# Column sums of squares as three bf16 parts, and a half tile of tokens filled up with zero rows, in a fused attention and feed-forward kernel

## The chip, the cores and the metric

The kernel runs on one core of one Trainium2 chip. Its time is the device time of one execution in microseconds (us). A profile shows the span from the first to the last instruction, which is some 1.8 us shorter than that time. PE is the tensor engine, PEld its weight loads, DVE the vector engine, ACT the scalar engine, POOL GpSimd, SP the engine that issues most DMAs.

## The reference, cut to what matters

```python
B, N, C = 4, 6080, 256
qn = q / (np.linalg.norm(q, axis=1, keepdims=True) + 1e-06)   # norm over the 6080 tokens, for each channel
kn = k / (np.linalg.norm(k, axis=1, keepdims=True) + 1e-06)
s = kn.transpose(0, 2, 1) @ qn / tau                          # 256 x 256 per batch
a = softmax(s)                                                # over the last axis
x = (v @ a).reshape(B * N, C)
out = gelu_tanh(x @ w_in) @ w_out                             # 256 -> 2048 -> 256
```

6080 tokens are 47 tiles of 128 and one of 64. That last one is the "half tile".

## The kernel before

The program runs in slots. In a slot PE does four matmuls of 512 columns (`hp`, the hidden layer), eight of 256 columns (`yp`, the output), and then one step of the attention of the next batch, from a Python generator: `yield` ends a step. So the attention of batches 1 to 3 hides nothing by itself; it is woven into the PE stream of the batch before. The parts that the change touches:

```python
def col_sums(cols, x, ones, first, last):
    for m in range(4):                       # q and k, two halves of 128 channels each
        nc.tensor.matmul(cols[:, m : m + 1],
                         lhsT=x[m // 2][:, m % 2 * 128 : m % 2 * 128 + 128], rhs=ones, ...)

def attention_steps(b, aw_next):
    ...
    for n, ch in enumerate(later_chunks):
        load_qk(b, n + 2)
        qk, whole = loaded_of.pop((b, n))
        for s, rows in slots_of(ch):         # rows: 128, or 64 for the half tile
            gram(G, qk, s, rows, first, last)              # two matmuls of 256 columns: G += k^T q
            flat = whole[:rows, :, s, :]
            ...                              # DVE: sq = flat * flat (bf16), acc += sq (fp32)
            yield
            ...
    cols = pA.tile([128, 512], FP32, tag="a", name="cols")
    col_sums(cols, [acc[:, x] for x in range(2)], ones_f, True, True)     # fp32 weights
    r = ...                                  # DVE copy; POOL: square root
    yield; yield; yield
    ...                                      # DVE: 1/norm; Gs = G scaled, fp32
    yield; yield
    T = turned(Gs)                           # four fp32 transposes on PE
    ...                                      # ACT: th; then per half jc, DVE: den, eT[jc]
    yield; yield
    rsinv = row_sums(eT)                     # rs: four matmuls of one column
    ...                                      # eight aw_part, one per slot
```

## Time and profile before

| What | Before |
|---|---|
| Time, median of the first 3 runs | 756.42 us (756.24 to 757.38) |
| PE busy in the stretch 41 to 712 us | 670.95 of 671.00 us |
| Slot with a gram of 128 rows / with the half tile | 1.96 / 2.16 us |
| fp32 column sums, per batch, on the PE stream | 0.81 us |
| DVE busy, ACT busy | 37%, 56% |

PE has no idle time in the middle of the run, so the only question for any change there is for how long it holds the PE stream. Such a hold is read from the distance of two starts in the timeline, not from the durations, which overlap. The lines are in the prediction below.

### The profile page before, as it was taken

What the parts mean: (1) busy time and instruction counts of PE and PEld (TensorE: products, weight loads), DVE (VectorE), ACT (ScalarE), POOL (GpSimd) and SP (SyncE); (2) the same over time, 40 slices, a digit from 0 to 9 for tenths busy, and PEclk for the clock granted to TensorE, in tenths of its full rate; (3) what the DMA queues carried; (4) which work ended last, traced back from release to release, by engine and by line L of the source; (5) the groups of instructions that cost most, each with busy time, mean ns of one, the idle gap of its engine ahead of it and who ended that gap; (6) DMA issues with size and microseconds to landing.
All of it is one profiled execution on the core that took longest, in us unless ns stands there. A gap on an engine that the chain in (4) does not pass through costs nothing.

```text
span 754.2 us, 12371 instructions
## 1 busy us (share of the span) xinstructions
PE 733.3 (97%) x5262; PEld 503.5 (67%) x5262; DVE 277.5 (37%) x485; ACT 420.3 (56%) x411; POOL 75.6 (10%) x150
## 2 busy tenths in 40 slices
PE   2999999999999999999999999999999999999998
PEld 1656666776666666776666666766767666666666
DVE  3733556454401546554521265555441011011011
ACT  4875555555456555555555555555546655555552
POOL 1311111101012102101001102010101000000000
PEclk9999999999999999999999999999999999999999
DMA  9999685615147685813435776661513543322111
GB/s 368 346 190 156 103 150 137 118 43 83 48 93 143 114 161 108 162 52 60 99 57 118 140 117 121 148 133 46 83 43 80 96 95 74 69 74 54 41 56 57
DMA packets 79639, 83.59 MB, mean 111 GB/s; under 512 B 55392, under 2 KB 59104, under 8 KB 79072
## 3 DMA queue, kind: packets, MB, share of 16 engines
q0 software_dynamic: 17104, 32.97, 27.4%
q1 hardware_dynamic: 62176, 48.20, 23.8%
q10 hardware_dynamic: 304, 1.64, 0.5%
q8 instruction: 41, 0.67, 0.4%
q14 instruction: 14, 0.11, 0.0%
HBM read 78.91 MB, written 24.90 MB: 138 GB/s over the span
## 4 chain that ended last, share of the span: by engine, by line
PE 94%; DMA 4%; ACT 1%; issue 0%; DVE 0%; SPq 0%; POOL 0%; DVEq 0%
PE yp L510 44%; PE hp L584 44%; PE G L157 4%; PE ps L217 2%; ACT sq L268 1%; DMA st<-in_q_dram 1%; DMA st<-in_k_dram 1%; DMA win_bf<-in_moe_w_in_dram 1%; PE cols L169 0%; PE yp L615 0%; PE T L195 0%; DVE aw L404 0%; PE vps L422 0%; PE ps L384 0%; PE rs L204 0%
## 5 line engine op out<-in xcount | busy, mean ns | idle before, releaser
L588 ACT ACTIVATE g<-hp 128x1024 bf16<-128x1024 f32 (+1 forms) x384 | 389.8, 1015 | 308.2 <-PE hp L584 308.2
L510 PE MATMUL yp<-wout_bf,g 128*128 128x256 bf16 x3024 | 392.0, 273 | 0.0
L584 PE MATMUL hp<-vT,aw 128*128 128x512 bf16 (+1 forms) x1536 | 390.8, 377 | 0.2 <-DVE aw L404 0.2
L510 PEld LDWEIGHTS <-g 128*128 128x128 bf16 x3024 | 295.9, 98 | 113.4
L584 PEld LDWEIGHTS <-aw 128*128 128x128 bf16 x1536 | 149.9, 98 | 104.7 <-issue 0.6
L527 DVE COPY ysb<-yp 128x512 f32<-128x512 f32 (+1 forms) x95 | 64.9, 683 | 402.5 <-PE yp L510 402.5
L451 DVE TENSOR_TENSOR acc<-acc,sq 128x512 f32<-128x512 f32 (+1 forms) x141 | 97.5, 692 | 4.8
L450 DVE TENSOR_TENSOR sq<-qkb 128x512 bf16<-128x512 bf16 (+1 forms) x141 | 58.7, 417 | 0.0
L157 PE MATMUL G<-qkb 128*128 128x256 bf16 (+1 forms) x288 | 55.0, 273 | 0.0
L308 POOL DMA_DIRECT2D vb<-in_v_dram x47 | 25.8, 551 | 76.6 <-DMA vT<-vb 64.3
L226 DVE TENSOR_SCALAR aw<-ps,rsinv 128x512 bf16<-128x512 f32 x30 | 22.4, 749 | 27.1 <-PE ps L217 26.7
L157 PEld LDWEIGHTS <-qkb 128*128 128x128 bf16 (+1 forms) x288 | 27.9, 98 | 3.8 <-issue 0.6
L333 POOL CAST gate<-g 1x1 f32<-1x1 bf16 x24 | 5.9, 244 | 237.3 <-ACT g L588 237.3
L157 PE MATMUL G<-qk 128*128 128x256 bf16 x96 | 13.7, 301 | 15.6 <-DVE qk L266 15.6
L268 ACT ACTIVATE sq<-st 128x3072 bf16<-128x3072 f32 (+2 forms) x9 | 21.1, 2379 | 11.2 <-DMA st<-in_q_dram 8.2
L157 PEld LDWEIGHTS <-qk 128*128 128x128 bf16 x96 | 9.9, 108 | 19.0 <-DVE qk L266 16.6
L266 DVE CAST qk<-st 128x3072 bf16<-128x3072 f32 (+2 forms) x10 | 14.2, 1437 | 13.2 <-DMA st<-in_q_dram 10.0
L217 PE MATMUL ps<-win_bf,eT 128*128 128x512 bf16 x60 | 17.7, 379 | 0.0
L461 POOL TENSOR_TENSOR r<-r,half 128x4 f32<-128x4 f32 x3 | 3.1, 1043 | 113.8 <-DVE r L460 113.8
L81 POOL DMA_DIRECT2D qkb<-in_q_dram x24 | 12.8, 535 | 6.8 <-issue 4.7
L81 POOL DMA_DIRECT2D qkb<-in_k_dram x24 | 12.9, 538 | 0.0
L567 POOL COPY g<-gr 128x1024 bf16<-128x1024 bf16 x2 | 2.1, 1036 | 105.1 <-PE yp L510 105.1
(69 smaller groups left out, 100.7 us busy)
## 6 DMA issues: line engine op xcount, KB each, us to landing
out_dram<-ysb SPq DMA_DIRECT2D x44, 512.0 KB, 2.9
vb<-in_v_dram POOLq DMA_DIRECT2D x43, 256.0 KB, 6.8
qkb<-in_q_dram POOLq DMA_DIRECT2D x21, 384.0 KB, 4.7
qkb<-in_k_dram POOLq DMA_DIRECT2D x21, 384.0 KB, 6.5
st<-in_q_dram SPq DMA_DIRECT2D x2, 1536.0 KB, 11.8
vT<-vb SPq DMA_TRANSPOSE x184, 3.0
st<-in_k_dram ACTq DMA_DIRECT2D x1, 1536.0 KB, 10.3
st<-in_k_dram SPq DMA_DIRECT2D x1, 1536.0 KB, 16.7
```

What stands on the lines that cost most here:

```text
L81: engines[x].dma_start(out=dst[x][:, 0:size, :], in_=src[b, s0 * 128 : (s0 + size) * 128, :].rearrange("(p s) c -> p s c", s=size))
L157: nc.tensor.matmul(G[:, ic, :], lhsT=qk[1][:rows, s, ic * 128 : ic * 128 + 128], rhs=qk[0][:rows, s, :], start=first and ic == 0, stop=las ...
L217: nc.tensor.matmul(ps, lhsT=eT[:, jc, ic * 128 : ic * 128 + 128], rhs=win_bf[:, jc, fs * 512 : fs * 512 + 512], start=jc == 0, stop=jc == 1)
L226: nc.vector.tensor_scalar_mul(dst, ps, scale)
L268: nc.scalar.activation(sq, x, AF.Square)
L308: nc.gpsimd.dma_start(out=t[:, 0:n, :], in_=v_rows[r0 : r0 + n * 128, :].rearrange("(p s) c -> p s c", s=n))
L450: nc.vector.tensor_mul(sq[:rows], flat, flat)
L451: nc.vector.tensor_add(acc[:rows], acc[:rows], sq[:rows])
L510: nc.tensor.matmul(yp[:rows, at, :], lhsT=g[:, fc, s * 128 : s * 128 + rows], rhs=wout_bf[:, fc, :], start=fc == 0, stop=fc == FC - 1)
L527: nc.vector.tensor_copy(ysb[:, s0 : s + 1, :], yp[:, 0 : s + 1 - s0, :])
L584: nc.tensor.matmul(hp[:, j, :cols], lhsT=aw[:, cc, fc * 128 : fc * 128 + 128], rhs=vT[:, cc, :cols], start=cc == 0, stop=cc == 1)
L588: nc.scalar.activation(g[:, 2 * i : 2 * i + 2, :cols], hp[:, :, :cols], AF.Gelu_apprx_tanh)
```

## The change

The intent: PE gets no fp32 weights for the column sums of batches 1 to 3. The fp32 sum `acc` is split into three bf16 numbers that add up to it, each is summed in bf16, and PSUM adds the three. Two empty slots give DVE time for the split. The half tile gets 64 zero rows, so that all its instructions have 128 rows.

```diff
@@ load_qk
+            if later_chunks[n][2]:
+                nc.gpsimd.memset(t[REM:, :, later_chunks[n][1], :], 0.0)
             load_chunk((nc.gpsimd, nc.gpsimd), views, b, later_chunks[n])
@@ attention_steps
-            for s, rows in slots_of(ch):
+            for s, rows in slots_of(ch, 128):
@@
+        parts = [split.tile([128, 2, 256], BF16, tag=f"part{n}", name="part") for n in range(3)]
+        nc.vector.tensor_copy(parts[0], acc)
+        nc.vector.tensor_sub(acc, acc, parts[0])
+        nc.vector.tensor_copy(parts[1], acc)
+        nc.vector.tensor_sub(parts[2], acc, parts[1])
+        yield
+        yield
         cols = pA.tile([128, 512], FP32, tag="a", name="cols")
-        col_sums(cols, [acc[:, x] for x in range(2)], ones_f, True, True)
+        for n, part in enumerate(parts):
+            col_sums(cols, [part[:, x] for x in range(2)], ones_bf, n == 0, n == 2)
```

(Cut: the pool of the parts is added, and the pool of `acc` goes from two buffers to one.)

## The prediction

> **What bounds the kernel now.** I read the page first: busy times, the 40 slices and the chain that ended last.
>
> ```profile
> PE 733.3 (97%) x5262; PEld 503.5 (67%) x5262; DVE 277.5 (37%) x485; ACT 420.3 (56%) x411; POOL 75.6 (10%) x150
> ...
> PE 94%; DMA 4%; ACT 1%; issue 0%; DVE 0%; SPq 0%; POOL 0%; DVEq 0%
> ```
>
> The tensor engine is the chain for 94% of the span, and in the slices it stands at 9 from the second slice to the last but one, at full granted clock. A busy matmul row alone proves little, because matmuls overlap, so I took the busy time by stretches: from 41 to 712 us PE is busy for 670.95 of 671.00 us. In that stretch nothing else decides the time. An instruction taken out of the PE stream shortens the run by the time for which it held the stream, and work added to another engine costs nothing unless it makes PE wait. The change touches batches 1 to 3 only, and their attention steps are woven into that stretch, from 66 to 560 us. The first batch (up to 41 us) and the tail are not touched.
>
> Next I read the timeline of PE alone around the column sums of batch 1. The columns are start, time from first start to last end, engine, line, operation, and count.
>
> ```profile
> 170.24 1.04 PE L510 MATMUL yp<-wout_bf,g 128*128 128x256 bf16 x8
> 171.11 0.95 PE L169 MATMUL cols<-ones_f,acc 128*128 128x1 f32 x8
> 171.92 1.02 PE L584 MATMUL hp<-vT,aw 128*128 128x512 bf16 x4
> 172.78 1.04 PE L510 MATMUL yp<-wout_bf,g 128*128 128x256 bf16 x8
> ```
>
> The second column overlaps the next row, so the cost of a block is the distance of two starts. The fp32 sums hold PE from 171.11 to 171.92: 0.81 us. The batches after it have the same (350.72 to 351.53, 532.07 to 532.89). Note "x8": the program issues four matmuls there, and the trace shows two passes for each.
>
> The same operation in bf16 is already in this trace, in the first batch:
>
> ```profile
> 30.46 1.05 PE L157 MATMUL G<-qk 128*128 128x256 bf16 x8
> 31.35 0.45 PE L169 MATMUL cols<-ones_bf,pair 128*128 128x1 bf16 x12
> 31.66 0.54 PE L169 MATMUL cols<-ones_bf,sq 128*128 128x1 bf16 x16
> 32.06 0.81 PE L153 MATMUL idle<-filler 128*128 128x512 bf16 x3
> ```
>
> Twelve bf16 sums hold PE for 31.66 - 31.35 = 0.31 us, and sixteen for 0.40 us: 25 to 26 ns each. Twelve is just what the changed kernel needs per batch (three parts by four column groups).
>
> Last, the weight loads around the half tile of batch 1, where the bracket gives idle time before the group and what ended it:
>
> ```profile
> 73.37 0.97 PEld L510 LDWEIGHTS <-g 128*128 128x128 bf16 x8
> ...
> 75.33 0.97 PEld L510 LDWEIGHTS <-g 128*128 128x128 bf16 x8
> 76.51 0.11 PEld L157 LDWEIGHTS <-qkb 64*128 64x128 bf16 x2 [0.21 <-issue]
> 76.83 0.55 PEld L584 LDWEIGHTS <-aw 128*128 128x128 bf16 x4 [0.21 <-issue]
> 77.49 0.97 PEld L510 LDWEIGHTS <-g 128*128 128x128 bf16 x8
> ```
>
> A slot with a full tile lasts 75.33 - 73.37 = 1.96 us, the slot with the 64-row tile 77.49 - 75.33 = 2.16 us. The difference stands at the two seams, where the weight load could not run ahead of the matmuls, and no semaphore is named. On PE itself the seams are about 0.10 and 0.11 us: the half tile starts at 76.51 after eight matmuls begun at 75.54 that elsewhere take 0.87 us (so 76.41), and the next group at 76.83 instead of 76.51 + 0.21 = 76.72. The list of waits has the same gap for all three batches (0.6 us in 3 for each seam, on the weight-load row).
>
> **What the Trainium skill says.** "TensorE: Matmul & The Clock Gate", section on Weight-path perf modes: fast weight load is on for 128 weights of a type that is not FP32. The trace agrees: one load record is 96 ns for the bf16 sums and 192 ns for the fp32 ones. "FP8 and Floating Point Precision", TensorE Precision Notes: true FP32 takes four passes through the array. The trace shows two records of load and of matmul per fp32 instruction, so it does not show four; I use the measured 0.81 us. "TensorEngine Tiling (Array Packing)", Key Properties: changing the tiling mode drains the engine. The trace agrees in kind, with the two 0.21 us gaps in the weight loads at the 64-row tile. "VectorE: DVE Perf Modes", the section on the TRN2 errata, gives (N+151)/0.96 ns for an fp32 two-tensor add, 691 ns at 512 elements; the adds into acc here take 692 ns.
>
> **The change part by part.** (1) It removes three blocks of fp32 sums and puts three blocks of twelve bf16 sums in: 3 x (0.81 - 0.31) = 1.50 us off the PE stream. The number of PE matmul records should rise by 36 - 24 = 12.
>
> (2) It makes the half tile a full one. The matmul streams 256 columns either way (274 against 273 ns), so only the seams go: 3 x (0.10 + 0.11) = 0.63 us off the PE stream. The three vector pairs on 64 rows become 128 rows at the same time (409 to 417 ns and 683 to 692 ns).
>
> (3) It adds four vector instructions a batch. An estimate from rows of this trace: a cast of 1024 fp32 takes 694 ns and one of 2048 takes 1226 ns, so 512 should take about 0.43 us; a two-tensor fp32 operation takes 0.69 us. 2 x 0.43 + 2 x 0.69 = 2.24 us. The last add ends at 168.47 and the sums now start two slots (3.5 us) after 171.1, so the parts are there by 170.8, some 3.5 us early. DVE is at 37% busy. Off the path.
>
> (4) It adds three memsets on POOL, of 64 partitions by 512 bf16, ahead of the load of the first chunk. The filler of the same width took 525 ns. The chunk's issue at 48.0 us then slips to 48.5; with a median landing time of 5.4 us (9.2 at most) it is there before the use at 66.5. Off the path.
>
> (5) It moves everything after the sums by two slots. That is the part to look at, because the copies of the output (ysb) come every four slots and keep their places: the order of the built programs shows one of them now standing between the two halves of eT, where before there was none. Before:
>
> ```profile
> 180.60 0.60 PE L195 MATMUL T<-ident,Gs 128*128 128x128 f32 x4
> ...
> 180.80 0.69 DVE L527 COPY ysb<-yp 128x512 f32<-128x512 f32 x1 [4.98 <-PE yp L510]
> ...
> 186.31 0.42 DVE L487 SCALAR_TENSOR_TENSOR eT<-th,den 128x256 bf16<-128x256 f32 x1
> ...
> 187.99 0.24 PE L204 MATMUL rs<-ones_bf,eT 128*128 128x1 bf16 x4
> ```
>
> eT is done at 186.73 and wanted at 187.99: 1.26 us of slack. In the changed kernel, count from the start of T. The copy has to wait for the end of the second slot after T: 0.44 + 2 x 1.74 = 3.92, plus the 0.20 us that such a copy starts later, 4.12. The next operation follows 0.60 us behind (as 174.46 follows 173.86), at 4.72, and the second half of eT takes 186.73 - 184.20 = 2.53 us: done at 7.25. It is wanted at 7.39, by the weight load at about 7.3. The slack falls from 1.26 us to between 0 and 0.15. I count a wait of 0 to 0.1 us a batch, 0.15 us in all.
>
> Sum: 1.50 + 0.63 - 0.15 = 1.98 us; 756.42 - 1.98 = 754.4 us, or 0.26% less.
>
> **The rivals.** First, the new vector order could become a wait. Against it: the arithmetic above gives next to nothing, and the other meeting point, Gs for T, keeps over a microsecond (the copy before it ends the wait, then 1.96 us from its start to the end of Gs, against some 3.3 to T). For it: the margin is that of two semaphores. Were each step 0.3 us later than I think, the loss is 3 x 0.3 = 0.9 us and the time 755.3. Second, the small bf16 sums could cost more in the middle of large matmuls than in the first batch, because a 26 ns matmul hides no weight load for the next hp block. If twelve cost 0.5 us, the gain falls to 3 x 0.31 + 0.63 = 1.56 and the time is 754.9. Against it: the stretch from sums to filler at 32.06 shows no such gap. Third, the drain at the half tile may not go away whole, as fp32 T and other kinds of matmul still mix: then 755.0. Fourth, nothing at all is gained because PE is waited for by something hidden behind it; 670.95 busy of 671.00 us speaks against this. No rival reaches 2%, which is 15 us.
>
> **Range and chances.** The three runs before span 1.1 us, which is over half of the effect, so the range has to hold that spread on top of the rivals: 753.0 to 756.2. A change of over 2% either way would need a lasting stall in every slot, and nothing in the build suggests one: faster 0.005, same 0.99, slower 0.005.
>
> **What would show it.** In the profile after: twelve bf16 sums on parts per batch, 0.31 us from the first to the next hp block; no 64-row form, and slots of 1.96 us throughout that stretch; no idle time on PE ahead of the sums; a wait of rs or its weight load for eT of at most 0.1 us, three times; the span near 752.2 against 754.2. It would be wrong if PE shows waits for DVE of several tenths at rs, if the twelve sums take over 0.5 us, or if the time stays above 756.2.

## The result

The changed kernel took 754.45 us (median of 4, 754.11 to 755.64) against 756.5 us before (median of 4): the ratio is 0.9974, with an interval of 0.9956 to 0.9991. Ratios here are the mean time of one kernel's fast runs over that of the other's of the same rounds, so not quite the ratio of the medians quoted. By the 2% line this is "the same"; the size is 2.05 us by the medians, where 1.98 was forecast.

First the page of the changed kernel, busy times and chain. PE is still the chain for 94% of the span. The weight loads went from 5262 to 5274 records: 36 - 24 = 12 more, as forecast. The matmul records fell (5262 to 5186) only because some are missing from this trace (`after_again`, the same kernel profiled once more, has 5274 of both), which is why I count loads.

```profile
PE 727.9 (97%) x5186; PEld 503.5 (67%) x5274; DVE 284.6 (38%) x497; ACT 420.1 (56%) x411; POOL 76.9 (10%) x153
...
PE 94%; DMA 4%; ACT 1%; issue 1%; SPq 0%; DVE 0%; POOL 0%
```

The timeline of PE around the sums of batch 1 (start, time from first start to last end, engine, line, operation, count):

```profile
175.28 1.04 PE L522 MATMUL yp<-wout_bf,g 128*128 128x256 bf16 x8
176.15 0.44 PE L170 MATMUL cols<-ones_bf,part 128*128 128x1 bf16 x12
176.46 1.02 PE L596 MATMUL hp<-vT,aw 128*128 128x512 bf16 x4
177.31 1.04 PE L522 MATMUL yp<-wout_bf,g 128*128 128x256 bf16 x8
```

The twelve sums hold PE for 176.46 - 176.15 = 0.31 us, where the fp32 block held it for 0.81. There is no idle bracket (the figure that names a wait) on them: the last part was ready at 172.41.

The weight loads at the former half tile (the sixth gram slot of batch 1):

```profile
77.11 0.97 PEld L522 LDWEIGHTS <-g 128*128 128x128 bf16 x8
78.09 0.21 PEld L158 LDWEIGHTS <-qkb 128*128 128x128 bf16 x2
78.30 0.64 PEld L596 LDWEIGHTS <-aw 128*128 128x128 bf16 x4
79.06 0.97 PEld L522 LDWEIGHTS <-g 128*128 128x128 bf16 x8
```

The two gaps of 0.21 us are gone, and the slot lasts 79.06 - 77.11 = 1.95 us like any other.

The timeline of all engines where the two extra slots left little room (the lines between are left out):

```profile
185.13 0.60 PE L196 MATMUL T<-ident,Gs 128*128 128x128 f32 x4
...
189.25 0.69 DVE L539 COPY ysb<-yp 128x512 f32<-128x512 f32 x1 [0.42 <-PE yp L522]
...
191.96 0.43 DVE L499 SCALAR_TENSOR_TENSOR eT<-th,den 128x256 bf16<-128x256 f32 x1
192.41 0.26 PEld L205 LDWEIGHTS <-eT 128*128 128x128 bf16 x4
192.52 0.24 PE L205 MATMUL rs<-ones_bf,eT 128*128 128x1 bf16 x4
...
193.05 1.02 PE L596 MATMUL hp<-vT,aw 128*128 128x512 bf16 x4
```

eT ended at 192.39, and its first load started at 192.41. No wait is named. (This first load needs only the first half of eT, and the loads of `yp` ahead of it end at 192.40. The load of the second half comes after it, so the room left is more than the 0.02 us that these two numbers suggest; `late_eT` below gives 0.07.) From the start of T to the hp block after rs is 7.92 us (185.13 to 193.05), and it was 7.92 us before (180.60 to 188.52); it is 7.92 us in the other two batches as well, before and after. So nothing was lost here, but next to nothing was left.

One thing in this profile does not fit: the span is 753.9 us, only 0.3 us below the 754.2 of before, where 752.2 was expected. The windows of the two kernels from 40 to 44 us tell where it is. Columns: the stretch, its length, busy time (and records) of PE, PEld, DVE, ACT and POOL, granted clock, DMA share, GB/s. Before:

```profile
40.00:44.00 4.00, 3.82 (x26) 1.93 (x24) 2.85 (x6) 3.02 (x5) 0.00 (x0) 1.00 1.24 199
```

After:

```profile
40.00:44.00 4.00, 3.44 (x18) 2.02 (x19) 1.57 (x4) 2.05 (x4) 0.00 (x0) 0.58 1.25 203
```

And PE's timeline there (with the last line of the run's `yp`, which is used below), before:

```profile
39.74 0.38 PE L384 MATMUL ps<-win_bf,eT 128*128 128x256 bf16 x2 [1.34 <-DMA win_bf<-in_moe_w_in_dram]
...
49.27 0.61 PE L422 MATMUL vps<-ident_bf,vb 128*128 128x128 bf16 x8
...
748.80 1.95 PE L615 MATMUL yp<-wout_bf,g 128*128 128x128 bf16 x32
```

After:

```profile
40.56 0.58 PE L387 MATMUL ps<-win_bf,eT 128*128 128x256 bf16 x2 [2.24 <-DMA win_bf<-in_moe_w_in_dram]
...
51.05 0.61 PE L425 MATMUL vps<-ident_bf,vb 128*128 128x128 bf16 x8
...
748.42 1.95 PE L627 MATMUL yp<-wout_bf,g 128*128 128x128 bf16 x32
```

In the profiled run the weights `win_bf` came 0.82 us later, PE waited 2.24 instead of 1.34 us, and in these 4 us the granted clock was 0.58. The first block that is the same in both runs (`vps`) starts at 51.05 instead of 49.27, 1.78 us late. The change edits nothing that runs before the first chunk's load, at 49.3 us here. The three other runs of the changed kernel had a mean clock of 1.000 and spans of 752.5, 752.9 and 752.3 us.

So I add a second measure, which leaves the start-up and the last DMAs out: the **woven stretch**, from the start of these `vps` matmuls to the start of the last row of outputs (`yp`, the group of 32 with 128 columns), read from the PE timeline of each profile. Before it is 748.80 - 49.27 = 699.53 us. After it is 748.42 - 51.05 = 697.37 us: 2.16 us less. The removed PE time, 3 x (0.81 - 0.31) + 3 x 0.21, makes 2.13.

### The profile page after: what moved, and what is told of

Its sections match the earlier page's. It is cut to its first block, busy times and chain, and to the rows that moved or that the text cites. A ratio compares the mean times of both kernels' runs of the same rounds, so it can differ in the third digit from the quotient of the medians.

```text
span 753.9 us, 12324 instructions
## 1 busy us (share of the span) xinstructions
PE 727.9 (97%) x5186; PEld 503.5 (67%) x5274; DVE 284.6 (38%) x497; ACT 420.1 (56%) x411; POOL 76.9 (10%) x153
## 4 chain that ended last, share of the span: by engine, by line
PE 94%; DMA 4%; ACT 1%; issue 1%; SPq 0%; DVE 0%; POOL 0%
PE yp L522 44%; PE hp L596 43%; PE G L158 4%; PE ps L218 2%; ACT sq L269 1%; DMA st<-in_q_dram 1%; DMA st<-in_k_dram 1%; DMA win_bf<-in_moe_w_in_dram 1%; PE ps L387 0%; PE yp L627 0%; PE T L196 0%; PE cols L170 0%; PE vps L425 0%; SPq L82 0%; PE rs L205 0%
## 5 line engine op out<-in xcount | busy, mean ns | idle before, releaser
L596 PE MATMUL hp<-vT,aw 128*128 128x512 bf16 (+1 forms) x1456 | 384.5, 377 | 3.6
L454 DVE TENSOR_TENSOR acc<-acc,sq 128x512 f32<-128x512 f32 x141 | 97.6, 692 | 4.8
L453 DVE TENSOR_TENSOR sq<-qkb 128x512 bf16<-128x512 bf16 x141 | 58.9, 418 | 0.0
L158 PE MATMUL G<-qkb 128*128 128x256 bf16 x288 | 55.0, 273 | 0.0
L158 PEld LDWEIGHTS <-qkb 128*128 128x128 bf16 x288 | 28.2, 98 | 3.3
```

The costliest lines, as they stand in the source:

```text
L158: nc.tensor.matmul(G[:, ic, :], lhsT=qk[1][:rows, s, ic * 128 : ic * 128 + 128], rhs=qk[0][:rows, s, :], start=first and ic == 0, stop=las ...
L453: nc.vector.tensor_mul(sq[:rows], flat, flat)
L454: nc.vector.tensor_add(acc[:rows], acc[:rows], sq[:rows])
L596: nc.tensor.matmul(hp[:, j, :cols], lhsT=aw[:, cc, fc * 128 : fc * 128 + 128], rhs=vT[:, cc, :cols], start=cc == 0, stop=cc == 1)
```

## The experiments

Eleven kernels ran, in four calls; kernels of one call share a chip and the runs of the kernel before. The last column compares woven stretches with the kernel before.

| Kernel | Median, us (range) | Before, same chip | Ratio, 95% interval | Woven stretch |
|---|---|---|---|---|
| parts_only | 755.27 (754.72 to 756.05) | 756.81 | 0.9980 (0.9968 to 0.9992) | -1.54 |
| zero_only | 755.97 (755.34 to 757.43) | 756.81 | 0.9991 (0.9979 to 1.0003) | -0.64 |
| after_again | 754.61 (754.31 to 756.60) | 756.81 | 0.9973 (0.9961 to 0.9986) | -2.16 |
| one_part_bf16_T | 753.38 (753.22 to 755.33) | 756.81 | 0.9961 (0.9949 to 0.9972) | -3.41 |
| no_extra_slots | 754.51 (753.78 to 756.67) | 756.68 | 0.9974 (0.9958 to 0.9991) | -2.16 |
| late_eT | 755.83 (755.58 to 757.31) | 756.93 | 0.9992 (0.9977 to 1.0007) | -0.63 |
| half_everywhere | 785.67 (785.36 to 786.10) | 756.93 | 1.0384 (1.0367 to 1.0402) | +29.37 |
| fp32_sums_x11 | 805.75 (804.99 to 807.86) | 756.93 | 1.0652 (1.0632 to 1.0672) | +49.72 |
| bf16_sums_x11 | 768.11 (766.17 to 769.15) | 756.93 | 1.0147 (1.0128 to 1.0166) | +10.06 |
| fp32_sums_x3 | 762.90 (762.04 to 767.65) | 758.00 | 1.0082 (1.0041 to 1.0122) | +5.36 |
| bf16_sums_x3 | 756.71 (756.24 to 759.19) | 758.00 | 0.9993 (0.9973 to 1.0013) | -0.36 |

### Each half of the change alone, and the whole again

`parts_only` is the changed kernel with the half tile back:

```diff
-            if later_chunks[n][2]:
-                nc.gpsimd.memset(t[REM:, :, later_chunks[n][1], :], 0.0)
-            for s, rows in slots_of(ch, 128):
+            for s, rows in slots_of(ch):
```

> The three bf16 parts and the two extra slots, but the half tile of 64 rows is back. Theory (two separate gains on the tensor engine's stream, 1.50 us from the sums and 0.63 us from the half tile's seams): 1.5 us less than the kernel before, some 0.6 us more than the changed kernel; the twelve sums hold PE for 0.31 us a batch and the slot of the half tile is 2.16 us again. Rival (the whole gain is of the sums, the zero rows give nothing): the same time as the changed kernel, 2.0 us less than before.

`zero_only` is the kernel before with only these lines of the change:

```diff
+            if later_chunks[n][2]:
+                nc.gpsimd.memset(t[REM:, :, later_chunks[n][1], :], 0.0)
-            for s, rows in slots_of(ch):
+            for s, rows in slots_of(ch, 128):
```

> The zero rows alone, with the fp32 sums and without the extra slots. Theory: 0.6 us less than the kernel before; every slot with a gram 1.95 us, the fp32 block still 0.81 us. Rival (zero rows give nothing): the time of the kernel before.

`after_again` is the changed kernel without an edit.

> The changed kernel once more, on the same chip as the others of this call and with more rounds. Both theories: 2.0 us less than the kernel before, 754.4. A profile without the dip of the clock at 40 to 44 us should show a span about 1.8 us shorter than the 753.9 us of the first profile, that is about 752.2.

The woven stretches are -1.54 and -0.64 us for the halves and -2.16 for the whole: the two gains are separate and add up (2.18). The rival that gives the zero rows nothing falls by the stretch. By the times alone it would not fall, because the interval of zero_only includes 1. The repeat of the changed kernel gave the same stretch to the hundredth (697.37 us), though its profiled run again had a late start: its six times lie in two groups, 754.3 to 754.7 and 756.4 to 756.6, and the profiled run is of the second group, with `vps` at 51.84 us and a mean clock of 0.998. So the expected span of 752.2 us did not come (754.7).

The other profiles show that the cause lies outside the change. Of the 13 profiled runs, five have a lower clock from 40 to 44 us (0.57 to 0.79), and in these `vps` starts at 51.05 to 51.84 us; in the other eight it starts at 49.24 to 50.06. One of the five, fp32_sums_x3 (below), has nothing of the change in it. The late weights alone do not do it: with the first `win_bf` matmul at 40.34 us and the clock at 1.00, bf16_sums_x3 reached `vps` at 49.87; with it at 40.45 and 0.64, fp32_sums_x3 reached it at 51.31. What makes the weights late and the clock fall there stays open. For runs without a profile the mean clock does not tell the two groups apart: the four short runs of after_again have 0.997 to 1.000.

### The half tile, everywhere

```diff
-                gram(G, qk, s, rows, first, last)
+                gram(G, qk, s, 64, first, last)
```

> The kernel before with every one of the 49 gram slots of the later batches on 64 rows only (a wrong result on purpose). Theory (the seam costs 0.21 us whenever a 64-row tile stands between 128-row ones): 3 x 48 x 0.21 = 30 us more than the kernel before; each slot 2.16 us. Rival (the 0.21 us at the one half tile was of its place, a late load or the like): no more than 1 us.

The weight loads of this kernel, two slots:

```profile
67.68 0.97 PEld L510 LDWEIGHTS <-g 128*128 128x128 bf16 x8
68.86 0.11 PEld L157 LDWEIGHTS <-qkb 64*128 64x128 bf16 x2 [0.21 <-issue]
69.18 0.55 PEld L584 LDWEIGHTS <-aw 128*128 128x128 bf16 x4 [0.21 <-issue]
69.85 0.97 PEld L510 LDWEIGHTS <-g 128*128 128x128 bf16 x8
```

Each slot now has both gaps and lasts 69.85 - 67.68 = 2.17 us. The trace has 288 such loads, 144 slots, of which three were half tiles before too (there are 48 gram slots a batch, not the 49 of the expectation). So 141 more such slots cost 29.37 us, 0.208 us each. The 0.21 us belong to the change between 128 and 64 rows and not to the place of the one half tile. (The G of this kernel is wrong on purpose. The comparison with the reference passed it all the same, which shows that the outputs depend little on G here; it is a weak test of anything in G.)

### The cost of the sums, multiplied

```diff
-        col_sums(cols, [acc[:, x] for x in range(2)], ones_f, True, True)
+        for _ in range(11):
+            col_sums(cols, [acc[:, x] for x in range(2)], ones_f, True, True)
```

> The kernel before with its fp32 column sums done eleven times over in the same slot (same result). Theory (the block of four fp32 sums holds PE for 0.81 us, without hiding in anything): 3 x 10 x 0.81 = 24.3 us more than the kernel before. Rival (part of the 0.81 us is a switch of type at its edges, paid once per block): clearly less, for example 18 us if a quarter of a microsecond is the edge.

`bf16_sums_x11` does the same with the loop over the three parts of the changed kernel.

> The changed kernel with its twelve bf16 sums done eleven times over (same result). Theory (twelve hold PE for 0.31 us): 3 x 10 x 0.31 = 9.3 us more than the changed kernel, 7.2 us more than the kernel before. Rival (small matmuls cost more amid large ones, 0.5 us for twelve): 15 us more than the changed kernel.

Both missed: 48.8 us more than the kernel before where 24.3 was expected, and 13.5 us more than the changed kernel's 754.61 (of another chip; 12.2 by the stretches) where 9.3 was. The windows of fp32_sums_x11 show why (columns as above):

```profile
170.00:174.00 4.00, 4.00 (x36) 3.44 (x33) 0.00 (x0) 1.44 (x2) 0.00 (x0) 1.00 0.00 0
174.00:176.00 2.00, 2.00 (x19) 2.00 (x20) 0.00 (x0) 0.00 (x0) 0.00 (x0) 0.97 0.00 0
176.00:180.00 4.00, 4.00 (x20) 4.00 (x20) 0.00 (x0) 0.00 (x0) 0.00 (x0) 0.50 0.02 4
```

The 88 passes began at 171.80. After about 4 us the granted clock fell to one half, and it stayed there until after the large matmuls were back, at 186.72. PE stands as busy for all of this. The bf16 block is shorter: its 132 matmuls held PE for 3.31 us. The clock did not fall in batch 1; it fell just after the block in batch 2 (0.58 in 362 to 366 us) and 0.3 us before its end in batch 3 (0.75 in 546 to 548 us). In the three batches together the longer bf16 blocks account for about 3 x 3.0 = 9.0 of the 12.2 us, and the clock for the rest. So a multiplied experiment must stay short, and these two runs could not tell edge from body. I took them again threefold.

> The eleven-fold sums brought the granted clock down to one half, so their time says little of one block. [...] The kernel before with its fp32 sums three times over: in the eleven-fold run 33 passes took 3 us at full clock, 0.091 us each, 0.73 us for the eight of a block. Theory now (0.73 us a block and 0.08 us once at its edges): the block holds PE for 0.08 + 3 x 0.73 = 2.26 us, 4.4 us in all more than the kernel before. Theory of before (0.81 us, no edge): 2.43 us and 4.9 us more. If the clock falls again: 6 us or more.

> The changed kernel with its twelve bf16 sums three times over. In the eleven-fold run 132 held PE for 3.31 us, 25 ns each. Theory: 36 hold PE for 0.91 us, 1.8 us more than the changed kernel, at full clock throughout. Rival (the clock falls after these too): 3 us more or above, with a lower granted clock in the slots that follow.

fp32_sums_x3, PE:

```profile
172.28 1.04 PE L511 MATMUL yp<-wout_bf,g 128*128 128x256 bf16 x8
173.15 2.74 PE L169 MATMUL cols<-ones_f,acc 128*128 128x1 f32 x24
175.75 1.02 PE L585 MATMUL hp<-vT,aw 128*128 128x512 bf16 x3
```

bf16_sums_x3, PE:

```profile
174.97 1.04 PE L170 MATMUL cols<-ones_bf,part 128*128 128x1 bf16 x36
175.87 1.02 PE L597 MATMUL hp<-vT,aw 128*128 128x512 bf16 x3
```

In both profiled runs the clock was full around the sums. (One unprofiled run of each had a lower mean clock, 0.991 with 767.65 us and 0.995 with 759.19 us; the stretches are of the profiled ones.) The bf16 reading was right: 36 hold PE for 0.90 us, and the stretch is 697.37 + 1.80 us. For fp32 both expectations were too low: 24 passes held PE for 2.60 us. Sixteen more passes cost 2.60 - 0.81 = 1.79 us, 0.112 us each, and the stretch agrees (5.36 / 48 = 0.112). My 0.091 was a misreading: a window counts every record that touches it, and a record of 0.25 us touches two. The one block of the kernel before, 0.81 us, is therefore cheaper than eight such passes (0.90) by 0.09 us. An edge that costs extra is ruled out. The trace of before shows where the 0.09 us are. Among its weight loads is this group:

```profile
171.00 0.97 PEld L169 LDWEIGHTS cols<-ones_f,acc 128*128 128x128 f32 x8
```

The first load starts at 171.00, 0.11 us ahead of the first sum and under the yp matmuls. The eight passes start at 171.11, 171.14 and then every 0.11 us, so the first holds PE for only 0.03 us and the other seven for 0.112 each, which makes 0.81.

"TensorE: Matmul & The Clock Gate" in the Trainium skill gives, in its section LDWEIGHTS, columns / 1.2 in ns for a load, which makes an estimate of 107 ns for 128 columns; and in the section "Wait — 56ns, not 53.3ns?" a floor of about 25 ns between starts of small matmuls. The fp32 passes and their loads, 112 ns apart, come near the first, and the bf16 sums, 25 ns apart, agree with the second. But each bf16 sum loads 128 columns too, and in the changed kernel these loads also start 25 ns apart, so the first figure does not hold for bf16 loads here.

### One more vector operation ahead of eT, and no extra slots

late_eT puts a subtraction between the two halves of eT; its result is not used:

```diff
                 yield
+                if jc == 1:
+                    nc.vector.tensor_sub(acc, acc, parts[1])
                 nc.vector.tensor_scalar(den[:, jc, :], th[:, jc, :], -1.0, 1.0,
```

> The changed kernel with one more vector subtraction of 0.69 us (its result is not used) between the two halves of eT. Theory (the moved output copy has used up the slack there to 0.02 us, so any more shows up on PE): rs waits about 0.7 us in each of three batches, 2.1 us more than the changed kernel, which brings it back to the kernel before. Rival (the margin in the trace is only how the records look, some tenths of slack are left): 1 us more or less.

Its weight loads at rs:

```profile
190.81 0.10 PEld L205 LDWEIGHTS <-eT 128*128 128x128 bf16 x1
191.44 0.14 PEld L205 LDWEIGHTS <-eT 128*128 128x128 bf16 x3 [0.53 <-DVE eT L501]
```

The first load needs only the first half of eT and goes at once; the second waits for the other half, and DVE is named. The subtraction delays the end of eT, counted from T, from 7.26 us (185.13 to 192.39) to 7.84 us (183.54 to 191.38). The stretch grew by 1.53 us against the changed kernel, 0.51 us a batch. So of 0.58 us all but 0.07 reached PE. The theory holds in kind: the slack is used up to less than a tenth of a microsecond. The expected 2.1 us was too large, as the next vector instruction follows this one after 0.60 us (188.25 to 188.85) and not after 0.69, and as 0.07 us of slack was left and not 0.02. The rival, some tenths of slack, is out.

no_extra_slots takes the two slots away again:

```diff
         nc.vector.tensor_sub(parts[2], acc, parts[1])
-        yield
-        yield
```

> The changed kernel without the two slots between the split and the sums. The split ended at 172.41 in the changed kernel and the sums' old place comes at 172.68, its weight load at about 172.57. Theory: the parts are just in time (margin some 0.1 us), no wait on PE, the slack of eT is 1.2 us again, and the time is that of the changed kernel within 0.3 us. Rival (the two slots were needed): PE waits for DVE ahead of the sums, 0.3 to 1 us a batch, 1 to 3 us more than the changed kernel.

Its DVE, the last instruction of the split and the next one:

```profile
170.00 0.69 DVE L465 TENSOR_TENSOR part<-acc,part 128x512 bf16<-128x512 f32 x1
171.44 0.16 DVE L470 COPY r<-cols 128x4 f32<-128x4 f32 x1 [0.74 <-PE cols L170]
```

Its PE:

```profile
170.08 1.04 PE L520 MATMUL yp<-wout_bf,g 128*128 128x256 bf16 x8
170.96 0.44 PE L170 MATMUL cols<-ones_bf,part 128*128 128x1 bf16 x12
171.26 1.02 PE L594 MATMUL hp<-vT,aw 128*128 128x512 bf16 x3
```

The split ended at 170.69 and the sums started at 170.96, at 170.08 + 0.87 as if nothing had been waited for. The stretch is the same as that of the changed kernel. The two slots were not needed, and without them eT has its old place against the output copies.

### Going on in the same direction

one_part_bf16_T keeps one bf16 part instead of three, no extra slots, and turns Gs in bf16:

```diff
-        (three parts: copy, subtract, copy, subtract; two yields)
+        parts = [split.tile([128, 2, 256], BF16, tag="part0", name="part")]
+        nc.vector.tensor_copy(parts[0], acc)
...
-        Gs = scaled(G, r)
+        Gs = scaled(G, r, BF16)
-        T = turned(Gs)
+        T = turned(Gs, BF16)
```

> A version that goes on where the theory points: one bf16 part instead of three (4 sums a batch, not exact any more), no extra slots, and the four fp32 transposes T of the later batches in bf16. Theory (only the tensor engine's stream counts, 26 ns per small bf16 matmul): 3 x 8 x 0.026 = 0.6 us from the sums, and T from 0.44 to 0.22 us a batch (as the eight bf16 transposes of v took 0.45 us) 0.65 us: 1.3 us less than the changed kernel, about 753.2. Rival (the stream has slack elsewhere and has given all there is): the time of the changed kernel. The result must still agree with the reference.

Its PE at the sums and at T:

```profile
171.68 0.24 PE L170 MATMUL cols<-ones_bf,part 128*128 128x1 bf16 x4
171.78 1.02 PE L591 MATMUL hp<-vT,aw 128*128 128x512 bf16 x4
...
180.47 0.39 PE L196 MATMUL T<-ident_bf,Gs 128*128 128x128 bf16 x4
180.69 1.03 PE L591 MATMUL hp<-vT,aw 128*128 128x512 bf16 x4
```

Four sums hold PE for 0.10 us and the transposes for 0.22 us, as expected. The stretch is 1.25 us shorter than that of the changed kernel, and the time is 753.38 against 754.61 us. It is the fastest of these kernels, and it agreed with the reference. The two parts of this step were not run apart; they are separate only in the PE lines above. The sums are no longer exact by design, and half_everywhere showed that this comparison says little about errors in G or the norms; whoever keeps it should check those by themselves.

## Why the prediction was right

**What bounds the kernel** held. In every experiment the change of the woven stretch could be read off PE: as a hold, as a wait, or as a lower clock. The time, 754.45 us, is within the range. That 2.05 us by the medians lies so close to 1.98 is in part luck: the interval of the ratio allows 0.7 to 3.3 us. The stretches and the PE lines carry the parts below.

**(1) The sums, 1.50 us**: 1.52 by stretch (zero_only against the whole), 1.54 (parts_only). The step that carried it was to look for the same operation in the trace of before, where twelve bf16 sums had been measured in the first batch (0.31 us, the same as later on parts). It held amid large matmuls too, so the second rival (0.5 us for twelve) is out.

**(2) The half tile, 0.63 us**: 0.64 alone, 0.62 as the last step. The third rival, a drain that does not go away whole, is out: the slot is 1.95 us.

**(3) The split, 2.24 us of DVE**: 170.08 to 172.41 in the changed kernel, 2.33 us, ready 3.7 us before the sums. Off the path, as said. It would have been off the path without the extra slots too, which I had not asked.

**(4) The memsets** took 0.520 us each (0.525 estimated) and nothing waited for them.

**(5) The move of eT** was the right place to look: the order of the built programs and rows of the old trace gave the end of eT at 7.25 us after T, and it came at 7.26. The term made from it was mis-sized: 0.15 us of waits were counted, and there were none. That is the whole difference between the forecast 1.98 us and the 2.16 us of the stretch, with some hundredths of rounding.

**What was to be seen** came as listed, but for the span. "The span near 752.2" failed in the one profiled run, because I had allowed for a spread of the times but not of the span that goes with one of them. What went with it was a late load of `win_bf` and a clock of 0.58 after it, which other profiles have too, and the six times of after_again lie in two groups some 2 us apart. That is as large as the effect, so a single profile before and after, compared by span, would have said 0.3 us.

## What to carry to other kernels

Where one engine has no idle time, value a change by the distance of starts that it takes from that engine's stream, and look first whether the trace already holds the new form of the operation somewhere. Compare kernels over a stretch between two fixed instructions when the start-up varies by as much as the effect. Before adding slots "to be safe", look what else they move: here they were not needed and used up 1.2 us of slack elsewhere.

## What the Trainium skill lacked or had wrong

- "FP8 and Floating Point Precision", TensorE Precision Notes, says four passes for true FP32. The trace has two records of load and matmul for each fp32 sum (24 for 12), and one for each fp32 transpose (T: 4 for 4), so the prediction's "two per fp32 instruction" holds for the sums alone. Four bf16 sums took 0.10 us and four fp32 ones 0.81 us in place, or 0.90 us repeated.
- "TensorEngine Tiling (Array Packing)", Key Properties, says that a change of mode drains the engine, without a cost. Here going from 128 to 64 rows and back costs 0.208 us a slot over 141 slots, about 0.1 us each way.
- "TensorE: Matmul & The Clock Gate", Part 1, ties the halved clock to idle time. Here the granted clock fell to 0.50 after about 4 us of one-column fp32 matmuls, with PE shown as busy for the whole time, and it fell in two of three batches 3 to 4 us after a block of one-column bf16 matmuls had begun. The page does not say whether such matmuls count as activity.
